# Head pairs mixed side by side in column tiles, and q cast straight into DRAM scratch, in a one-core Sinkhorn-attention and SwiGLU kernel

## The chip, the cores and the metric

The kernel runs on one core of one Trainium2 chip. The metric is device time in microseconds (us); lower is better. The runs of the kernel before scatter over about 2%. A run more than 1.5% above the fastest of its kernel counts as slow, and comparisons use fast runs alone.

Names of engines: PE is TensorE, DVE is VectorE, ACT is ScalarE, POOL is GpSimd, SP ("sync") is SyncE. DMAs issued by SP go through the hardware queue; those issued by POOL, which are the ones that cast fp32 to bf16, go through the software queue.

## The reference, cut to what matters

```python
B, H, S, D = 4, 8, 768, 64;  n_blocks = 8;  block = 96
P = sort_net                                   # (B, H, 8, 8); five rounds of exp and row/column normalisation
k_sorted = einsum('bhij,bhjcd->bhicd', P, k_blocks)      # each block becomes a mix of the 8 blocks
v_sorted = einsum('bhij,bhjcd->bhicd', P, v_blocks)
attn = softmax(q_block @ k_sorted_block.T / 8) @ v_sorted_block      # within a block of 96
x = attn heads side by side                    # (3072, 512)
out = (silu(x @ w_gate) * (x @ w_val)) @ w_out # d_ff 1536
```

## The kernel before, the parts that matter

The work runs in eight windows, two halves (of 384 tokens) for each of four batches. A window does the gate and value matmuls of its half, then the output matmuls of the half before; the attention of the next half and the preparation of the next batch are woven in between. Batch 0 is prepared by PE alone. Batches 1 to 3 go through DRAM scratch: k and v are mixed on PE (64 partitions each, one per head and block), written to scratch, and come back transposed by DMA (`kqt`, for k and q) or re-laid (`vt`, the value tile).

```python
def load_later(b):                                        # POOL, casts fp32 -> bf16
    load(kv[b][0:R], k_nat[b]); load(kv[b][R:2 * R], v_nat[b])
    for two in range(2):
        load(q_sb[b][two * 32:(two + 1) * 32], qv[two])
load_later(1); load(wo_sb, wo_dram); load_later(2); load_later(3)

def later_q(b):                                           # sync: q from SBUF to scratch, runs of 128 B
    qs = dram.tile([H2, NB, C, 2, D], BF16)
    for two in range(2):
        nc.sync.dma_start(out=qs[:, :, :, two]..., in_=q_sb[b][two * 32:(two + 1) * 32])

def one(c0, c):                                           # later_mix: 12 matmuls of 128x512 a batch
    nc.tensor.matmul(mp, lhsT=kvmix[b], rhs=kv[b][:, c:c + 8, :], ...)
    drain(m_sb[:, c - c0:c - c0 + 8], mp)                 # DVE and ACT in turn
    if c + 8 == c0 + CB:                                  # sync: k and v to scratch, runs of 128 B
        ...

def later_back(b):                                        # sync
    for a, t in ((1, "q"), (0, "k")):
        for g in range(H2):
            nc.sync.dma_start_transpose(out=kqt[:, a, g]..., in_=scr[(t, b)][g]...)
    nc.sync.dma_start(out=vt[:, :, 0:D], in_=scr[("v", b)]...)     # 6144 runs of 128 B
# ... cut ...
for w, (b, half) in enumerate(win):
    main = gv_steps(b, half)
    if w > 0: main = main + out_steps(*win[w - 1])
    if half == 0:
        sides.append((att_steps(b, 1), 0, n - 2))
        later_q(b + 1); sides.append((later_mix(b + 1), lo, lo + 6)); sides.append((later_back..., lo + 7, lo + 8))
    elif b + 1 < B:
        sides.append((att_steps(b + 1, 0), 1, n - 1))
    merge(main, *sides)
```

`merge` gives the order in which the program is written. A scheduler then reorders it when the kernel is built, by its own estimate of when each input is ready. PE executes that built order strictly: in the trace it stands 22.1 us at one matmul that waits, and does nothing that is written behind it.

The softmax here doesn't subtract the row's maximum and nothing guards it: scores larger than these inputs give would overflow.

Of the kernel before, what the change touches and what calls it, by code (L numbers as in the profile page):

```python
# [9 lines left out]
FP32 = mybir.dt.float32  # L10
BF16 = mybir.dt.bfloat16
AF = mybir.ActivationFunctionType
ALU = mybir.AluOpType
# [4 lines left out]
def kernel(  # L18
# [11 lines left out]
    nc = tc.nc  # L30

    B, H, S, D = q.shape
    NB = sort_net.shape[-1]
    C = S // NB
    BH = B * H
    H2 = H // 2
# [7 lines left out]
    R = H * NB  # L44
# [9 lines left out]
    const = ctx.enter_context(tc.tile_pool(name="const", bufs=1))  # L54
    natp = ctx.enter_context(tc.tile_pool(name="natp", bufs=1))
    mixp = ctx.enter_context(tc.tile_pool(name="mixp", bufs=2))
    kqp = ctx.enter_context(tc.tile_pool(name="kqp", bufs=2))
    vtp = ctx.enter_context(tc.tile_pool(name="vtp", bufs=2))
    epool = ctx.enter_context(tc.tile_pool(name="epool", bufs=8))
    ssp = ctx.enter_context(tc.tile_pool(name="ssp", bufs=3))  # L60
# [5 lines left out]
    psum = ctx.enter_context(tc.tile_pool(name="psum", bufs=3, space=bass.MemoryType.PSUM))  # L66
    dram = ctx.enter_context(tc.tile_pool(name="dram", bufs=1, space=bass.MemoryType.DRAM))
# [6 lines left out]
    kq0 = natp.tile([128, C, D], BF16, name="kq0", tag="nat", bufs=3)  # L74
    v0 = natp.tile([128, 128, D], BF16, name="v0")
    kv = [None] * B
    q23 = natp.tile([128, C, D], BF16, name="q23")
    q_sb = [None, v0[R:2 * R, 0:C], q23[0:R], q23[R:2 * R]]
    nc.vector.memset(v0[0:R, C:, :], 0.0)

    def load(dst, src):
        nc.gpsimd.dma_start(out=dst, in_=src)
# [25 lines left out]
    rmix = const.tile([128, 2, 2, H2, NB], BF16, name="rmix")  # L108
    vmix = const.tile([R, 2, H2, NB], BF16, name="vmix")

    kvmix = [None] + [const.tile([128, 2, 2, H2, NB], BF16, name=f"kvmix{b}") for b in range(1, B)]
    idq = ident[R:2 * R, R:2 * R].rearrange("p (g two j) -> p two g j", two=2, j=NB)
    nc.vector.memset(rmix, 0.0)
    nc.vector.tensor_copy(rmix[R:2 * R, :, 1, :, :], idq)
    for b in range(1, B):
        nc.vector.memset(kvmix[b], 0.0)

    for s in range(4):
        load(v0[s * 16:(s + 1) * 16, 0:C], v_nat[0, s * 16:(s + 1) * 16])
# [24 lines left out]
    for two in range(2):  # L144
# [1 line left out]
            rmix[0:R, two, 0],  # L146
            mask[0:R].rearrange("p (g two) -> p two g", two=2)[:, two].unsqueeze(2).to_broadcast([R, H2, NB]),
            wk, op=ALU.mult)
    nc.vector.tensor_copy(vmix, rmix[0:R, :, 0])
    for b in range(1, B):  # L150
        for t in range(2):
            rows = slice(t * R, (t + 1) * R)
            nc.vector.tensor_tensor(
                kvmix[b][rows, t].rearrange("p two g i -> p g two i"),
                mask[rows].rearrange("p (g two) -> p g two", two=2).unsqueeze(3).to_broadcast([R, H2, 2, NB]),
                w_ps[rows, :, b].unsqueeze(1).unsqueeze(1).to_broadcast([R, H2, 2, NB]), op=ALU.mult)

    for m in range(0, DF, 256):
        load(wg_sb[:, :, m:m + 256], wg_dram[:, :, m:m + 256])
        load(wv_sb[:, :, m:m + 256], wv_dram[:, :, m:m + 256])  # L160

    def load_later(b):
        kv[b] = natp.tile([128, C, D], BF16, name=f"kv{b}", tag="nat", bufs=3)
        load(kv[b][0:R], k_nat[b])
        load(kv[b][R:2 * R], v_nat[b])
        qv = q[b].rearrange("(g two) (j c) d -> two g j c d", two=2, c=C)
        for two in range(2):
            load(q_sb[b][two * 32:(two + 1) * 32], qv[two])

    load_later(1)  # L170
    load(wo_sb, wo_dram)
    load_later(2)
    load_later(3)

    tog = [0]

    def drain(dst, src):
        if tog[0] % 2 == 0:
            nc.vector.tensor_copy(dst, src)  # L179
        else:  # L180
            nc.scalar.copy(dst, src)  # L181
        tog[0] += 1
# [2 lines left out]

    def new_vt(b):

        vt = vtp.tile([C, H * NB, D + 1], BF16, name=f"vt{b}", tag="vt")
        nc.vector.memset(vt[:, :, D:D + 1], 1.0)
        vts[b] = vt  # L190
        return vt

# [15 lines left out]
            drain(dst[:, :, ts(cb, 8)], tp.transpose([0, 2, 1]))  # L208

    def first_v():  # L210
        dst = new_vt(0)
        for db in range(D // 8):
            tp = psum.tile([128, 8, H * NB], FP32, name="tv", tag="att")
            for ld in range(8):
                nc.tensor.matmul(tp[:, ld], lhsT=v0[0:R, :, db * 8 + ld],  # L215
                                 rhs=vmix.rearrange("p two g i -> p (two g i)"),
                                 start=True, stop=True)
            drain(dst[:, :, ts(db, 8)], tp[0:C].transpose([0, 2, 1]))



    scr = {}

    def later_q(b):
        qs = dram.tile([H2, NB, C, 2, D], BF16, name=f"qs{b}")
        for two in range(2):
            nc.sync.dma_start(out=qs[:, :, :, two].rearrange("g i c d -> (g i) c d"),
                              in_=q_sb[b][two * 32:(two + 1) * 32])
        scr[("q", b)] = qs

    def later_mix(b):

        ks = dram.tile([H2, NB, C, 2, D], BF16, name=f"ks{b}")
        vs = dram.tile([C, 2, H2, NB, D], BF16, name=f"vs{b}")
        scr[("k", b)], scr[("v", b)] = ks, vs
        steps = []
        CB = 48
        m_of = {}

        def one(c0, c):  # L240
            if c == c0:
                m_of[c0] = mixp.tile([128, CB, D], BF16, name="m_sb", tag="mix")
            m_sb = m_of[c0]
            mp = psum.tile([128, 8, D], FP32, name="mp", tag="att")
            nc.tensor.matmul(mp.rearrange("p a b -> p (a b)"),  # L245
                             lhsT=kvmix[b].rearrange("p a two g i -> p (a two g i)"),
                             rhs=kv[b][:, c:c + 8, :].rearrange("p a b -> p (a b)"),
                             start=True, stop=True)
            drain(m_sb[:, c - c0:c - c0 + 8], mp)
            if c + 8 == c0 + CB:  # L250
                for two in range(2):
                    nc.sync.dma_start(  # L252
                        out=ks[:, :, c0:c0 + CB, two].rearrange("g i c d -> (g i) c d"),
                        in_=m_sb[two * 32:(two + 1) * 32])
                nc.sync.dma_start(
                    out=vs[c0:c0 + CB].rearrange("c two g i d -> (two g i) c d"), in_=m_sb[R:2 * R])

        for c0 in range(0, C, CB):
            for c in range(c0, c0 + CB, 8):
                steps.append(lambda c0=c0, c=c: one(c0, c))  # L260
        return steps

    def later_back(b):
        kqt = new_kqt(b)
        for a, t in ((1, "q"), (0, "k")):
            s = scr[(t, b)].rearrange("g i c two d -> g (i c) (two d)")
            for g in range(H2):
                nc.sync.dma_start_transpose(out=kqt[:, a, g].rearrange("p i c -> p (i c)"), in_=s[g])  # L268
        vt = new_vt(b)
        nc.sync.dma_start(out=vt[:, :, 0:D],  # L270
                          in_=scr[("v", b)].rearrange("c two g i d -> c (two g i) d"))

    es_of = {}
    xts = {}
# [17 lines left out]
    def av(b, half, g):  # L292
        if g == 0:
            xts[(b, half)] = xtp.tile([128, H2, TW], BF16, name=f"xt{b}_{half}", tag="xt")
        xt, vt, es = xts[(b, half)], vts[b], es_of[(b, half, g)]
        av_ps = psum.tile([C, 2, 512], FP32, name="av_ps", tag="av", bufs=1)
        avv = av_ps[:, :, 0:4 * (D + 1)].rearrange("p two (i e) -> p two i e", e=D + 1)
        for two in range(2):
            for i4 in range(4):
                nc.tensor.matmul(avv[:, two, i4, :], lhsT=es[two][:, i4, :],  # L300
                                 rhs=vt[:, (two * H2 + g) * NB + half * 4 + i4, :],
                                 start=True, stop=True)
        r_sb = ssp.tile([C, 2, 4, 1], FP32, name="r_sb", tag="r")
        nc.vector.reciprocal(r_sb, avv[:, :, :, D:D + 1])  # L304
        st = ssp.tile([C, 4, 2, D], BF16, name="st", tag="st")
        nc.vector.tensor_tensor(st.rearrange("p i two d -> p two i d"), avv[:, :, :, 0:D],  # L306
                                r_sb.to_broadcast([C, 2, 4, D]), op=ALU.mult)
        x_ps = psum.tile([128, 4, C], BF16, name="x_ps", tag="att")
        for i4 in range(4):
            nc.tensor.transpose(x_ps[:, i4, :], st[:, i4].rearrange("p a b -> p (a b)"),  # L310
                                ident[0:C, 0:C])
        drain(xt[:, g, :], x_ps.rearrange("p a b -> p (a b)"))
# [78 lines left out]
    for w, (b, half) in enumerate(win):  # L391
        main = gv_steps(b, half)
        if w > 0:
            main = main + out_steps(*win[w - 1])
        n = len(main)
        sides = []
        if half == 0:
            sides.append((att_steps(b, 1), 0, n - 2))
            if b + 1 < B:
                later_q(b + 1)  # L400
                lo = 4 if w == 0 else 0
                sides.append((later_mix(b + 1), lo, lo + 6))
                sides.append(([lambda b=b: later_back(b + 1)], lo + 7, lo + 8))
        elif b + 1 < B:
            sides.append((att_steps(b + 1, 0), 1, n - 1))
        merge(main, *sides)
# [30 lines left out]
```

## Time and profile before

| | before |
|---|---|
| median of 3 runs | 323.8 us (323.37 to 324.45) |
| span of the profiled run | 321.9 us |
| PE restarts with batch 1's scores / first values of batch 1 are used | 108.95 us / 123.07 us |
| values to the end | 198.8 us |

In the page's slices (40 of about 8 us; busy tenths, and for PEclk the granted clock in tenths of full speed) PE has a hole from about 87 to 123 us, and the DMA engines are nearly full until about 80 us, at 7 tenths in most of the hole, and full again at its end, while the values are loaded:

```profile
PE   0377999999700105999999999999999799999995
...
PEclk9995579999955555599999999999999769999999
DMA  6999999999777799028799432697971000020022
```

The list of PE's waits (engine, instruction, what it waited for: us in total, times, longest) names what ended the hole: first the transposed k of batch 1, then its value tile. The line between them lies in the start of the program and is 12.5 us.

```profile
PE qk_1054 L284 <- DMA kqt_1011<-ks_666: 22.1, 1, 22.1
PE w_ps L140 <- DVE lmix L134: 12.5, 1, 12.5
PE av_ps L300 <- DMA vt_1020<-vs_667: 12.1, 1, 12.1
```

Sync's own timeline (start, us, engine, line, operation) shows the series behind it. The first issue waits for q's load until 52.8 us; its two stores of q are accepted only by 85.3 us, because the issuing queue is held while the DMA engines are busy with the loads. The mixed k and v, ready at about 61 us, stand behind them.

```profile
52.83 32.46 SPq L227 DMA_DIRECT2D qs_663<-v_99  x2
85.40 5.22 SPq L252 DMA_DIRECT2D ks_666<-m_sb  x2
90.67 0.99 SPq L255 DMA_DIRECT2D vs_667<-m_sb  x1
91.76 4.10 SPq L252 DMA_DIRECT2D ks_666<-m_sb  x2
95.90 1.58 SPq L255 DMA_DIRECT2D vs_667<-m_sb  x1
97.58 7.78 SPq L268 DMA_TRANSPOSE kqt_1011<-qs_663  x4
105.47 5.18 SPq L268 DMA_TRANSPOSE kqt_1011<-ks_666  x4
110.70 0.62 SPq L270 DMA_DIRECT2D vt_1020<-vs_667  x1
```

The two queues' packets (count, MB, share of the 16 engines' time), and the value loads of batches 1 to 3 (KB, us from issue to landing):

```profile
q1 hardware_dynamic: 96864, 20.46, 43.2%
q0 software_dynamic: 10000, 14.16, 29.2%
...
vt_1020<-vs_667 SPq DMA_DIRECT2D x1, 768.0 KB, 12.3
vt_1678<-vs_1404 SPq DMA_DIRECT2D x1, 768.0 KB, 12.7
vt_2463<-vs_2189 SPq DMA_DIRECT2D x1, 768.0 KB, 12.8
```

The last view cuts the time behind the arrival of the values into four stages: to the fifth attention step of batch 1 (the first of its second half), to that of batch 2, to that of batch 3, and to the end. Columns: stretch, length, busy us of each engine with counts, granted clock, DMA share and GB/s.

```profile
123.10:136.20 13.10, 11.82 (x88) 6.92 (x88) 5.98 (x13) 4.71 (x11) 0.00 (x0) 0.50 0.44 75
136.20:196.50 60.30, 59.25 (x438) 33.27 (x437) 36.60 (x75) 26.18 (x56) 0.00 (x0) 1.00 0.73 105
196.50:259.90 63.40, 61.55 (x441) 34.45 (x439) 36.50 (x74) 26.61 (x57) 0.00 (x0) 0.94 0.61 88
259.90:321.90 62.00, 58.17 (x356) 31.17 (x352) 29.54 (x58) 19.58 (x40) 0.00 (x0) 0.97 0.10 39
```

### The profile page before, as it was taken

How to read it: one execution, taken by the hardware profiler on the slowest of the kernel's cores; microseconds unless marked ns; L12 is line 12 of the kernel's file. 1: busy time of each engine (PE TensorE's matmuls, PEld its weight loads, DVE VectorE, ACT ScalarE, POOL GpSimd, SP SyncE). 2: the span in 40 equal slices, each digit the busy share in tenths (PEclk: the TensorE clock that was granted, in tenths of full speed). 3: DMA queues.
4: the chain of work that ended last, by engine and by line, in shares of the span. 5: the costliest groups of instructions: out<-in, count | busy, mean ns of one | idle time of the engine just before them, and what ended most of it. 6: DMA issues, size and time to landing. Idle time of an engine off the chain costs nothing.

```text
span 321.9 us, 5048 instructions
## 1 busy us (share of the span) xinstructions
PE 261.3 (81%) x2004; PEld 150.9 (47%) x2004; DVE 163.7 (51%) x353; ACT 112.9 (35%) x234; POOL 23.9 (7%) x43
## 2 busy tenths in 40 slices
PE   0377999999700105999999999999999799999995
PEld 0367555555300103556555555554554556555542
DVE  6844368888000002578438447890880558628600
ACT  2153346433200201455233346632333345333321
POOL 8554301000000000000000000000000000000000
PEclk9995579999955555599999999999999769999999
DMA  6999999999777799028799432697971000020022
GB/s 106 193 180 200 217 143 148 192 188 171 124 122 140 141 92 199 0 38 132 144 117 112 107 105 38 101 124 149 98 122 65 35 0 3 0 98 2 0 98 98
DMA packets 106886, 34.93 MB, mean 109 GB/s; under 512 B 94960, under 2 KB 102640, under 8 KB 106224
## 3 DMA queue, kind: packets, MB, share of 16 engines
q1 hardware_dynamic: 96864, 20.46, 43.2%
q0 software_dynamic: 10000, 14.16, 29.2%
q8 instruction: 15, 0.25, 0.3%
q14 instruction: 7, 0.06, 0.1%
HBM read 30.68 MB, written 13.37 MB: 137 GB/s over the span
## 4 chain that ended last, share of the span: by engine, by line
PE 76%; DMA 8%; SPq 7%; DVE 4%; ACT 2%; issue 1%; POOL 0%; ACTq 0%; POOLq 0%
PE v_ps L343 20%; PE o_ps L354 19%; PE g_ps L334 19%; PE av_ps L300 5%; SPq L268 4%; DMA vt_1020<-vs_667 4%; PE x_ps L310 3%; PE mp L245 3%; DVE st L306 3%; DMA v_99<-in_v_dram 2%; SPq L252 2%; PE tv L215 2%; DMA kq_98<-in_k_dram 1%; PE tkq L205 1%; DVE r_sb L304 1%
## 5 line engine op out<-in xcount | busy, mean ns | idle before, releaser
L339 DVE SCALAR_TENSOR_TENSOR gs_sb<-th_sb,g_ps 128x384 bf16<-128x384 bf16 x96 | 52.9, 553 | 39.0 <-ACT th_sb L337 34.4
L337 ACT ACTIVATE th_sb<-g_ps 128x384 bf16<-128x384 f32 x96 | 47.0, 492 | 60.6 <-PE g_ps L334 59.0
L343 PEld LDWEIGHTS <-wv_sb 128*128 128x128 bf16 x384 | 37.5, 99 | 26.9 <-issue 2.5
L334 PEld LDWEIGHTS <-wg_sb 128*128 128x128 bf16 x384 | 37.3, 102 | 24.8 <-issue 3.7
L304 DVE RECIPROCAL r_sb<-av_ps 96x8 f32<-96x8 f32 x32 | 6.4, 201 | 71.0 <-PE av_ps L300 70.9
L357 ACT COPY o_sb<-o_ps 128x512 f32<-128x512 f32 x24 | 14.1, 586 | 46.8 <-PE o_ps L354 46.8
L306 DVE TENSOR_TENSOR st<-av_ps,r_sb 96x512 bf16<-96x512 f32 x32 | 21.9, 684 | 0.8
L284 PE MATMUL qk_1054<-kqt_1011 64*96 64x96 bf16 x4 | 0.6, 286 | 22.1 <-DMA kqt_1011<-ks_666 22.1
L310 PE MATMUL x_ps<-ident,st 96*128 96x96 bf16 x128 | 12.4, 228 | 4.2 <-DVE st L306 3.7
L310 PEld LDWEIGHTS <-st 96*128 96x128 bf16 x128 | 8.3, 106 | 15.3 <-DVE st L306 13.8
L284 PEld LDWEIGHTS <-kqt_1011 64*96 64x96 bf16 x64 | 3.0, 158 | 25.4 <-DMA kqt_1011<-ks_666 23.6
L334 PE MATMUL g_ps<-xt_0_558,wg_sb 128*128 128x384 bf16 x48 | 13.7, 373 | 0.1
L179 DVE CAST m_sb<-mp 128x512 bf16<-128x512 f32 x18 | 12.0, 683 | 3.4 <-PE mp L245 3.1
L334 PE MATMUL g_ps<-xt_0_2682,wg_sb 128*128 128x384 bf16 x48 | 12.9, 364 | 0.7 <-ACT o_sb L357 0.6
L334 PE MATMUL g_ps<-xt_0_1112,wg_sb 128*128 128x384 bf16 x48 | 12.9, 357 | 0.0
L343 PE MATMUL v_ps<-xt_0_558,wv_sb 128*128 128x384 bf16 x48 | 12.1, 361 | 0.1
L181 ACT CAST m_sb<-mp 128x512 bf16<-128x512 f32 x18 | 10.6, 590 | 4.4 <-PE mp L245 4.4
L343 PE MATMUL v_ps<-xt_0_2682,wv_sb 128*128 128x384 bf16 x48 | 11.5, 355 | 0.0
L334 PE MATMUL g_ps<-xt_0_1897,wg_sb 128*128 128x384 bf16 x48 | 11.2, 325 | 0.1
L343 PE MATMUL v_ps<-xt_0_1112,wv_sb 128*128 128x384 bf16 x48 | 11.2, 343 | 0.0
L140 PE MATMUL w_ps<-selb,lmix 32*64 32x4 bf16 x16 | 0.6, 190 | 12.5 <-DVE lmix L134 12.5
L343 PE MATMUL v_ps<-xt_0_1897,wv_sb 128*128 128x384 bf16 x48 | 10.4, 326 | 0.0
(368 smaller groups left out, 446.2 us busy)
## 6 DMA issues: line engine op xcount, KB each, us to landing
out_dram<-o_sb SPq DMA_DIRECT2D x24, 256.0 KB, 2.0
wg_sb<-in_moe_w_gate_dram POOLq DMA_DIRECT2D x6, 256.0 KB, 10.6
wv_sb<-in_moe_w_val_dram POOLq DMA_DIRECT2D x6, 256.0 KB, 10.5
wo_sb<-in_moe_w_out_dram POOLq DMA_DIRECT2D x1, 1536.0 KB, 30.9
q_100<-in_q_dram POOLq DMA_DIRECT2D x4, 384.0 KB, 33.8
kq_98<-in_k_dram POOLq DMA_DIRECT2D x4, 192.0 KB, 5.9
kq_98<-in_q_dram POOLq DMA_DIRECT2D x4, 192.0 KB, 6.8
v_99<-in_v_dram POOLq DMA_DIRECT2D x4, 192.0 KB, 9.5
```

What stands on the lines that cost most here:

```text
L179: nc.vector.tensor_copy(dst, src)
L181: nc.scalar.copy(dst, src)
L268: nc.sync.dma_start_transpose(out=kqt[:, a, g].rearrange("p i c -> p (i c)"), in_=s[g])
L300: nc.tensor.matmul(avv[:, two, i4, :], lhsT=es[two][:, i4, :], rhs=vt[:, (two * H2 + g) * NB + half * 4 + i4, :], start=True, stop=True)
L306: nc.vector.tensor_tensor(st.rearrange("p i two d -> p two i d"), avv[:, :, :, 0:D], r_sb.to_broadcast([C, 2, 4, D]), op=ALU.mult)
L310: nc.tensor.transpose(x_ps[:, i4, :], st[:, i4].rearrange("p a b -> p (a b)"), ident[0:C, 0:C])
L334: nc.tensor.matmul(g_ps, lhsT=wg_sb[:, kc, ts(m, 128)], rhs=xt[:, kc, :], start=(kc == 0), stop=(kc == NKC - 1))
L337: nc.scalar.activation(th_sb, g_ps, AF.Tanh, scale=0.5)
L339: nc.vector.scalar_tensor_tensor(gs_sb, th_sb, 1.0, g_ps, op0=ALU.add, op1=ALU.mult)
L343: nc.tensor.matmul(v_ps, lhsT=wv_sb[:, kc, ts(m, 128)], rhs=xt[:, kc, :], start=(kc == 0), stop=(kc == NKC - 1))
L354: nc.tensor.matmul(o_ps, lhsT=h_w[:, m, ts(t3, 128)], rhs=wo_sb[:, m, :], start=(m == 0), stop=(m == NFC - 1))
L357: nc.scalar.copy(o_sb, o_ps)
```

## The change

Intent: fewer small DMA pieces and no q store in sync's way. Mixing leaves each head pair side by side, so a k or v row of scratch is one run of 6 KB; q is cast by its load straight into DRAM scratch; the value load has 256 B runs. For this, mixing uses four column tiles of 32 per PSUM bank.

```diff
-    load(q_sb[b][two * 32:(two + 1) * 32], qv[two])
+    qs = dram.tile([H2, S, 2, D], BF16, name=f"qs{b}")
+    load(qs[:, :, two].rearrange("g s d -> s g d"), qv[two])          # 6144 pieces: 256 B read, 128 B written
-    later_q(b + 1)                                                    # the q stores on sync are gone
 # later_mix
-    nc.tensor.matmul(mp..., lhsT=kvmix[b]... , rhs=kv[b][:, c:c + 8, :]...)
-    drain(m_sb[:, c - c0:c - c0 + 8], mp)
+    for two in range(2):
+        for t in range(4):
+            c = t * CT + s * 8
+            nc.tensor.matmul(mp[t * 32:(t + 1) * 32]..., lhsT=kvmix[b][rows, two]..., rhs=kv[b][rows, c:c + 8, :]...)
+        drain(m_sb[:, s * 8:s * 8 + 8, two], mp)
+    for t in range(4):                                                # once per k and per v: 32 rows of 6 KB
+        nc.sync.dma_start(out=sc[a, :, :, t * CT:(t + 1) * CT]..., in_=m_sb[t * 32:(t + 1) * 32]...)
 # later_back
-    vt [C, H * NB, D + 1];  out=vt[:, :, 0:D]        (6144 runs of 128 B)
+    vt [C, H2 * NB, 2 * D + 2];  out=vt[:, :, 1:2 * D + 1]   (3072 runs of 256 B, rows of 260 B)
-    sides.append((later_back, lo + 7, lo + 8))
+    sides.append((later_back, lo + 6, lo + 7))
 # cut: mixing weights, first values, and the value matmuls follow the new layout
```

More of the change, by code (lines that the diff above doesn't have):

```diff
@@ L76 @@
     kv = [None] * B
-    q23 = natp.tile([128, C, D], BF16, name="q23")
-    q_sb = [None, v0[R:2 * R, 0:C], q23[0:R], q23[R:2 * R]]
     nc.vector.memset(v0[0:R, C:, :], 0.0)
@@ L109 @@
     vmix = const.tile([R, 2, H2, NB], BF16, name="vmix")
-    kvmix = [None] + [const.tile([128, 2, 2, H2, NB], BF16, name=f"kvmix{b}") for b in range(1, B)]
+    kvmix = [None] + [const.tile([128, 2, H2, NB], BF16, name=f"kvmix{b}") for b in range(1, B)]
+    mask2 = const.tile([128, 2, H2], BF16, name="mask2")
+    mrow = mask.rearrange("p (g two) -> p two g", two=2)
+    nc.vector.tensor_copy(mask2[0:R], mrow[0:R])
+    for two in range(2):
+        nc.vector.tensor_copy(mask2[R:2 * R, two], mrow[R:2 * R, 1 - two])
     idq = ident[R:2 * R, R:2 * R].rearrange("p (g two j) -> p two g j", two=2, j=NB)
@@ L114 @@
     nc.vector.tensor_copy(rmix[R:2 * R, :, 1, :, :], idq)
-    for b in range(1, B):
-        nc.vector.memset(kvmix[b], 0.0)
     for s in range(4):
@@ L148 @@
             wk, op=ALU.mult)
-    nc.vector.tensor_copy(vmix, rmix[0:R, :, 0])
+    for two in range(2):
+        nc.vector.tensor_copy(vmix[:, two], rmix[0:R, 1 - two, 0])
     for b in range(1, B):
-        for t in range(2):
-            rows = slice(t * R, (t + 1) * R)
-            nc.vector.tensor_tensor(
-                kvmix[b][rows, t].rearrange("p two g i -> p g two i"),
-                mask[rows].rearrange("p (g two) -> p g two", two=2).unsqueeze(3).to_broadcast([R, H2, 2, NB]),
-                w_ps[rows, :, b].unsqueeze(1).unsqueeze(1).to_broadcast([R, H2, 2, NB]), op=ALU.mult)
+        nc.vector.tensor_tensor(
+            kvmix[b], mask2.unsqueeze(3).to_broadcast([128, 2, H2, NB]),
+            w_ps[:, :, b].unsqueeze(1).unsqueeze(1).to_broadcast([128, 2, H2, NB]), op=ALU.mult)
     for m in range(0, DF, 256):
@@ L160, with load_kv @@
         load(wv_sb[:, :, m:m + 256], wv_dram[:, :, m:m + 256])
-    def load_later(b):
+    scr = {}
+    def load_kv(b):
         kv[b] = natp.tile([128, C, D], BF16, name=f"kv{b}", tag="nat", bufs=3)
@@ L165, in load_later, with load_q @@
         load(kv[b][R:2 * R], v_nat[b])
-        qv = q[b].rearrange("(g two) (j c) d -> two g j c d", two=2, c=C)
+    def load_q(b):
+        qs = dram.tile([H2, S, 2, D], BF16, name=f"qs{b}")
+        qv = q[b].rearrange("(g two) s d -> two s g d", two=2)
         for two in range(2):
-            load(q_sb[b][two * 32:(two + 1) * 32], qv[two])
-    load_later(1)
+            load(qs[:, :, two].rearrange("g s d -> s g d"), qv[two])
+        scr[("q", b)] = qs.rearrange("g (i c) two d -> g i c two d", c=C)
+    load_kv(1)
+    load_q(1)
     load(wo_sb, wo_dram)
-    load_later(2)
-    load_later(3)
+    for b in range(2, B):
+        load_kv(b)
+        load_q(b)
     tog = [0]
@@ L186, in new_vt @@
     def new_vt(b):
-        vt = vtp.tile([C, H * NB, D + 1], BF16, name=f"vt{b}", tag="vt")
-        nc.vector.memset(vt[:, :, D:D + 1], 1.0)
+        vt = vtp.tile([C, H2 * NB, 2 * D + 2], BF16, name=f"vt{b}", tag="vt")
+        nc.vector.memset(vt[:, :, 0:2 * D + 2:2 * D + 1], 1.0)
         vts[b] = vt
@@ L210, in first_v @@
     def first_v():
-        dst = new_vt(0)
+        dst = new_vt(0)[:, :, 1:2 * D + 1].rearrange("c gi (two d) -> c two gi d", two=2)
         for db in range(D // 8):
@@ L217, in first_v @@
                                  start=True, stop=True)
-            drain(dst[:, :, ts(db, 8)], tp[0:C].transpose([0, 2, 1]))
-    scr = {}
-    def later_q(b):
-        qs = dram.tile([H2, NB, C, 2, D], BF16, name=f"qs{b}")
-        for two in range(2):
-            nc.sync.dma_start(out=qs[:, :, :, two].rearrange("g i c d -> (g i) c d"),
-                              in_=q_sb[b][two * 32:(two + 1) * 32])
-        scr[("q", b)] = qs
-    def later_mix(b):
-        ks = dram.tile([H2, NB, C, 2, D], BF16, name=f"ks{b}")
-        vs = dram.tile([C, 2, H2, NB, D], BF16, name=f"vs{b}")
-        scr[("k", b)], scr[("v", b)] = ks, vs
-        steps = []
-        CB = 48
-        m_of = {}
-        def one(c0, c):
-            if c == c0:
-                m_of[c0] = mixp.tile([128, CB, D], BF16, name="m_sb", tag="mix")
-            m_sb = m_of[c0]
-            mp = psum.tile([128, 8, D], FP32, name="mp", tag="att")
-            nc.tensor.matmul(mp.rearrange("p a b -> p (a b)"),
-                             lhsT=kvmix[b].rearrange("p a two g i -> p (a two g i)"),
-                             rhs=kv[b][:, c:c + 8, :].rearrange("p a b -> p (a b)"),
-                             start=True, stop=True)
-            drain(m_sb[:, c - c0:c - c0 + 8], mp)
-            if c + 8 == c0 + CB:
-                for two in range(2):
-                    nc.sync.dma_start(
-                        out=ks[:, :, c0:c0 + CB, two].rearrange("g i c d -> (g i) c d"),
-                        in_=m_sb[two * 32:(two + 1) * 32])
-                nc.sync.dma_start(
-                    out=vs[c0:c0 + CB].rearrange("c two g i d -> (two g i) c d"), in_=m_sb[R:2 * R])
-        for c0 in range(0, C, CB):
-            for c in range(c0, c0 + CB, 8):
-                steps.append(lambda c0=c0, c=c: one(c0, c))
-        return steps
@@ new lines, in first_v, with one @@
+            drain(dst[:, :, :, ts(db, 8)],
+                  tp[0:C].rearrange("c d (two gi) -> c two gi d", two=2))
+    def later_mix(b):
+        CT = C // 4
+        sc = dram.tile([2, H2, NB, C, 2, D], BF16, name=f"kvs{b}")
+        scr[("k", b)], scr[("v", b)] = sc[0], sc[1]
+        m_of = {}
+        def one(a, s):
+            rows = slice(a * R, (a + 1) * R)
+            if s == 0:
+                m_of[a] = mixp.tile([128, CT, 2, D], BF16, name="m_sb", tag="mix", bufs=3)
+            m_sb = m_of[a]
+            for two in range(2):
+                mp = psum.tile([128, 8, D], FP32, name="mp", tag="att")
+                for t in range(4):
+                    c = t * CT + s * 8
+                    nc.tensor.matmul(mp[t * 32:(t + 1) * 32].rearrange("p a b -> p (a b)"),
+                                     lhsT=kvmix[b][rows, two].rearrange("p g i -> p (g i)"),
+                                     rhs=kv[b][rows, c:c + 8, :].rearrange("p a b -> p (a b)"),
+                                     start=True, stop=True)
+                drain(m_sb[:, s * 8:s * 8 + 8, two], mp)
+            if s == CT // 8 - 1:
+                for t in range(4):
+                    nc.sync.dma_start(
+                        out=sc[a, :, :, t * CT:(t + 1) * CT].rearrange("g i c two d -> (g i) (c two d)"),
+                        in_=m_sb[t * 32:(t + 1) * 32].rearrange("p c two d -> p (c two d)"))
+        return [lambda a=a, s=s: one(a, s) for a in range(2) for s in range(CT // 8)]
@@ L269, in later_back @@
         vt = new_vt(b)
-        nc.sync.dma_start(out=vt[:, :, 0:D],
-                          in_=scr[("v", b)].rearrange("c two g i d -> c (two g i) d"))
+        nc.sync.dma_start(out=vt[:, :, 1:2 * D + 1],
+                          in_=scr[("v", b)].rearrange("g i c two d -> c (g i) (two d)"))
     es_of = {}
@@ L295, in av @@
         xt, vt, es = xts[(b, half)], vts[b], es_of[(b, half, g)]
-        av_ps = psum.tile([C, 2, 512], FP32, name="av_ps", tag="av", bufs=1)
-        avv = av_ps[:, :, 0:4 * (D + 1)].rearrange("p two (i e) -> p two i e", e=D + 1)
+        av_ps = psum.tile([C, 1024], FP32, name="av_ps", tag="av", bufs=1)
+        E = D + 1
         for two in range(2):
             for i4 in range(4):
-                nc.tensor.matmul(avv[:, two, i4, :], lhsT=es[two][:, i4, :],
-                                 rhs=vt[:, (two * H2 + g) * NB + half * 4 + i4, :],
+                o = i4 * E + (2 if two == 0 else 512)
+                lo = (1 - two) * E
+                nc.tensor.matmul(av_ps[:, o:o + E], lhsT=es[two][:, i4, :],
+                                 rhs=vt[:, g * NB + half * 4 + i4, lo:lo + E],
                                  start=True, stop=True)
-        r_sb = ssp.tile([C, 2, 4, 1], FP32, name="r_sb", tag="r")
-        nc.vector.reciprocal(r_sb, avv[:, :, :, D:D + 1])
+        sums = av_ps[:, 66:66 + 892].rearrange("p (two x) -> p two x", two=2)[:, :, 0:4 * E:E]
+        data = av_ps[:, 2:1024].rearrange("p (two x) -> p two x", two=2)[:, :, 0:4 * E].rearrange(
+            "p two (i e) -> p two i e", e=E)[:, :, :, 0:D]
+        r_sb = ssp.tile([C, 2, 4], FP32, name="r_sb", tag="r")
+        nc.vector.reciprocal(r_sb, sums)
         st = ssp.tile([C, 4, 2, D], BF16, name="st", tag="st")
-        nc.vector.tensor_tensor(st.rearrange("p i two d -> p two i d"), avv[:, :, :, 0:D],
-                                r_sb.to_broadcast([C, 2, 4, D]), op=ALU.mult)
+        nc.vector.tensor_tensor(st.rearrange("p i two d -> p two i d"), data,
+                                r_sb.unsqueeze(3).to_broadcast([C, 2, 4, D]), op=ALU.mult)
         x_ps = psum.tile([128, 4, C], BF16, name="x_ps", tag="att")
@@ L399 @@
             if b + 1 < B:
-                later_q(b + 1)
                 lo = 4 if w == 0 else 0
                 sides.append((later_mix(b + 1), lo, lo + 6))
-                sides.append(([lambda b=b: later_back(b + 1)], lo + 7, lo + 8))
+                sides.append(([lambda b=b: later_back(b + 1)], lo + 6, lo + 7))
         elif b + 1 < B:
```

## The prediction

> **What bounds the kernel now.** The slice table shows TensorE (PE) at 90% or more from about 40 to 87 us and from about 124 us to the end. Between lies a hole: the list of PE waits gives 22.1 us for batch 1's first transposed K (PE restarts at 108.95 us) and 12.1 us for its values (to 123.07 us). The granted clock is 0.50 from 92 to 136 us. Outside the hole and the start PE waits a few us, so the time is: arrival of batch 1's values (123) plus about 200 us of PE work.
>
> The chain of waits and the sync queue's waits say why. Sync issues its DMAs in order; the first is the scratch store of q, which waits 51.7 us for q's cast load, to 52.8 us. That store, 2 x 3072 runs of 128 B, takes until about 90 us because cast loads (wo, later k, v, q) run beside it until about 81 us; in batch 3 it lands in 5.8 us. The Trainium skill, "DMA: Bandwidth & Descriptors", section "Queues, rings and completion order", says an engine takes turns between queues packet by packet; the trace agrees. Mixed k and v, ready at 61 us, are issued only at 85.4 (12 us of stores), then eight transposes (13 us), then the value load (12.3 us).
>
> **What changes.** Gone: q stores from SBUF (6144 packets a batch), nearly all 12288 k/v store packets (now 256 rows of 6 KB), half of the value load's (3072 of 256 B). Added: q's cast load becomes 6144 pieces, 256 B read and 128 B written, DRAM to DRAM, on the load queue. From 16 ns per packet and engine of the 128 B stores and 27 ns of the value load I estimate 20 to 30 ns each: 8 to 12 us a batch against about 5; the load queue ends near 100 us, not 81. On PE, mixing is 48 matmuls a batch, not 12; if groups of four overlap (Trainium skill, "TensorEngine Tiling (Array Packing)", "Tiling Modes": tiles work in parallel; no run shows it yet) it costs 1 to 2 us a batch, if not, 8 us. Evictions stay 12 of 128x512 (683 ns DVE, 590 ns ACT). The built order puts batch 1's first scores inside window (0,1), its first values after 20 of 36 output matmuls.
>
> **On the critical path.** q lands near 55 us; its transposes, ahead of the k/v stores, share the engines with wo and k2/v2, to about 80; stores to 86; K transposed near 90; the value load competes with q2 and k3/v3 and lands near 112 (98 to 122). The 34 us hole shrinks to some 25. Behind it stay about 200 us, plus 3 us of output matmuls moved behind it, plus 3 us of mixing.
>
> **Predicted: 317 us, 300 to 331 (8 in 10).** Faster by over 2%: 0.55; within 2%: 0.33; slower by over 2%: 0.12.
>
> **What would show it.** PE waits for batch 1's K and values shorter than 22 and 12 us; values at 105 to 118 us; sync's wait for q followed by transposes; hardware-queue packets down from 96864 to about 33000, load-queue packets up from 10000 to about 28000; mixing matmuls starting in overlapping fours. Wrong: values later than 120 us.
>
> **What would make it wrong.** Cast pieces over 35 ns each (slower), or well under 20 ns, or transposes that do not crawl beside the loads (300 or less); column tiles one after another (+16 us); sync holding output stores behind q2's transposes.

## The result, and the profile after

| | before | after |
|---|---|---|
| median, 4 runs each | 324.12 us (323.37 to 327.03) | 307.56 us (304.15 to 313.85) |
| ratio of fast runs | | 0.9438, 95% interval 0.9331 to 0.9546 |
| span of the profiled run | 321.9 us | 306.2 us |
| first values of batch 1 used | 123.1 us | 115.0 us |
| values to the end | 198.8 us | 191.2 us |

A ratio is the mean time of one kernel's fast runs over that of the other's in the same rounds, so it is not quite the ratio of the medians. The changed kernel is faster by 5.6%; I had forecast 317 us, 2.2% less than the 324.12 us measured beside it. The 307.56 lies inside the stated range, but the gain is far above the one forecast, and that is the error to explain.

The same views of the changed kernel. The hole in PE's row now begins near 76 us, and after 122 us the clock stays at full speed; before, it fell again near 250 us.

```profile
PE   0367999999000859999999999999999999999994
...
PEclk9995579999755595999999999999999999999999
DMA  6999999999999995045994010489500200010022
```

```profile
PE qk_1089 L282 <- DMA kqt_1031<-kvs_664: 22.6, 1, 22.6
...
PE av_ps L301 <- DMA vt_1040<-kvs_664: 3.2, 1, 3.2
```

PE's wait for k did not get shorter (22.6 us, before 22.1), because the built order brings PE to it at 76.4 us, not at 86.9 us; the wait for values fell from 12.1 to 3.2 us. Sync now begins with q's transposes. They take 26 us, and the k/v stores stand behind them:

```profile
47.80 26.25 SPq L266 DMA_TRANSPOSE kqt_1031<-qs_216  x4
74.15 8.38 SPq L255 DMA_DIRECT2D kvs_664<-m_sb  x8
91.77 7.99 SPq L266 DMA_TRANSPOSE kqt_1031<-kvs_664  x4
99.93 0.46 SPq L268 DMA_DIRECT2D vt_1040<-kvs_664  x1
```

```profile
q0 software_dynamic: 27664, 14.16, 38.5%
q1 hardware_dynamic: 33120, 18.10, 37.2%
...
vt_1040<-kvs_664 SPq DMA_DIRECT2D x1, 768.0 KB, 15.1
vt_1699<-kvs_1435 SPq DMA_DIRECT2D x1, 768.0 KB, 10.2
vt_2518<-kvs_2254 SPq DMA_DIRECT2D x1, 768.0 KB, 11.2
```

Packets on the hardware queue fell to a third and those on the load queue rose to 27,664, as forecast. With half the pieces batch 1's value load got longer (15.1 us, before 12.3), and those of batches 2 and 3 only 2.5 and 1.6 us shorter. The stages behind the values:

```profile
115.00:129.80 14.80, 14.29 (x127) 7.87 (x127) 6.96 (x15) 6.46 (x14) 0.00 (x0) 0.79 0.31 91
129.80:188.90 59.10, 58.99 (x475) 31.91 (x473) 36.71 (x76) 26.97 (x56) 0.00 (x0) 1.00 0.52 95
188.90:246.80 57.90, 57.75 (x458) 31.62 (x456) 35.76 (x73) 25.89 (x54) 0.00 (x0) 1.00 0.44 83
246.80:306.20 59.40, 55.42 (x351) 29.86 (x348) 28.39 (x56) 19.53 (x39) 0.00 (x0) 0.99 0.11 40
```

Set against the table before, the 15.7 us between the two spans split up without rest: arrival of the values 8.1 us earlier; first stage 1.7 us longer (it holds 16 output matmuls that stood ahead of the hole before); second stage 1.2 us, third 5.5 us, fourth 2.6 us shorter. So about half of the gain lies behind the values, most of it in the last two stages, where the change altered, besides the mixing, only the layout of the value tile and of the value matmuls' results (the normalising operation on DVE takes 686 ns in both kernels).

What did alter there is the built order. In the kernel before, batch 3's first four value steps stand behind all 36 output matmuls of the window, nearly back to back (before them stand 130.6, 130.6, 131.0 and 131.5 us of gate, value and output matmuls, counted at N columns / 2.4 GHz each). In the changed kernel these four stand at 112.8, 115.2, 117.8 and 121.6 us, with 2.4 to 3.8 us of long matmuls between one and the next, which PE can run while DVE normalises the step. This clock rate is from the Trainium skill, "Trainium Kernel Development and Optimization", section "NeuronCore Architecture"; the trace agrees (four matmuls of 384 columns take 0.65 us in the chain).

### The profile page after: what moved, and what is told of

The parts are those of the page before. It is cut to its first block, busy times and chain, and to the rows that moved or that the text cites. A ratio compares the mean times of both kernels' runs of the same rounds, so it can differ in the third digit from the quotient of the medians.

```text
span 306.2 us, 5232 instructions
## 1 busy us (share of the span) xinstructions
PE 257.5 (84%) x2103; PEld 145.8 (48%) x2112; DVE 163.2 (53%) x351; ACT 114.6 (37%) x234; POOL 32.3 (11%) x43
## 3 DMA queue, kind: packets, MB, share of 16 engines
q0 software_dynamic: 27664, 14.16, 38.5%
q1 hardware_dynamic: 33120, 18.10, 37.2%
## 4 chain that ended last, share of the span: by engine, by line
PE 60%; DMA 23%; SPq 12%; POOL 2%; issue 1%; ACT 1%; DVE 0%; POOLq 0%; ACTq 0%
PE o_ps L358 19%; PE g_ps L338 15%; PE v_ps L347 15%; SPq L266 11%; DMA qs_216<-in_q_dram 5%; DMA kvs_664<-m_sb 5%; DMA vt_1040<-kvs_664 5%; PE av_ps L301 4%; DMA wg_sb<-in_moe_w_gate_dram 4%; DMA v_99<-in_v_dram 3%; PE mp L248 2%; PE x_ps L314 2%; POOL kq_98 L80 1%; POOL qs_216 L80 1%; SPq L255 0%
## 5 line engine op out<-in xcount | busy, mean ns | idle before, releaser
L347 PEld LDWEIGHTS <-wv_sb 128*128 128x128 bf16 x384 | 37.4, 99 | 26.3 <-issue 2.9
L338 PEld LDWEIGHTS <-wg_sb 128*128 128x128 bf16 x384 | 35.1, 100 | 25.7 <-issue 7.4
L349 DVE SCALAR_TENSOR_TENSOR h_1_1073<-v_ps,gs_sb 128x384 bf16<-128x384 f32 x12 | 6.7, 558 | 24.3 <-PE v_ps L347 23.4
L282 PE MATMUL qk_1089<-kqt_1031 64*96 64x96 bf16 x4 | 0.6, 286 | 22.6 <-DMA kqt_1031<-kvs_664 22.6
L338 PE MATMUL g_ps<-xt_0_559,wg_sb 128*128 128x384 bf16 x48 | 13.3, 358 | 0.1
L314 PE MATMUL x_ps<-ident,st 96*128 96x96 bf16 x128 | 11.7, 217 | 1.2 <-DVE st L310 1.0
L347 PE MATMUL v_ps<-xt_0_559,wv_sb 128*128 128x384 bf16 x48 | 11.8, 354 | 0.0
L347 PE MATMUL v_ps<-xt_1_724,wv_sb 128*128 128x384 bf16 x48 | 11.4, 362 | 0.0
L338 PE MATMUL g_ps<-xt_1_724,wg_sb 128*128 128x384 bf16 x48 | 11.2, 357 | 0.0
L338 PE MATMUL g_ps<-xt_0_1147,wg_sb 128*128 128x384 bf16 x48 | 10.8, 327 | 0.0
L358 PE MATMUL o_ps<-wo_sb,h_0_679 128*128 128x512 bf16 x34 | 10.3, 449 | 0.3 <-issue 0.2
L338 PE MATMUL g_ps<-xt_0_1966,wg_sb 128*128 128x384 bf16 x48 | 10.5, 327 | 0.0
```

The lines of the kernel that those rows point to most:

```text
L314: nc.tensor.transpose(x_ps[:, i4, :], st[:, i4].rearrange("p a b -> p (a b)"), ident[0:C, 0:C])
L338: nc.tensor.matmul(g_ps, lhsT=wg_sb[:, kc, ts(m, 128)], rhs=xt[:, kc, :], start=(kc == 0), stop=(kc == NKC - 1))
L347: nc.tensor.matmul(v_ps, lhsT=wv_sb[:, kc, ts(m, 128)], rhs=xt[:, kc, :], start=(kc == 0), stop=(kc == NKC - 1))
L358: nc.tensor.matmul(o_ps, lhsT=h_w[:, m, ts(t3, 128)], rhs=wo_sb[:, m, :], start=(m == 0), stop=(m == NFC - 1))
```

## The experiments

Theories at the start: A, the built order and the density of PE's work set the time behind the values. B, the attention steps became cheaper by the new layout or by less DMA traffic.

### Order moved in the kernel before (spread3)

```diff
-    sides.append((att_steps(b + 1, 0), 1, n - 1))
+    sides.append((att_steps(b + 1, 0), 11, 15) if b == 2 else (att_steps(b + 1, 0), 1, n - 1))
+    # and each main step of that window is kept behind the value matmuls written before it
```

> The kernel before, with one thing changed: PE's order is held so that batch 3's first attention half lies between the last gate/value matmuls and the output matmuls of the window before it, instead of behind all of them. No DMA and no arithmetic changes. Theory A (what the prediction missed is PE work behind the values running at full clock instead of half, because dense matmuls stand between the attention steps): the stretch that ran at clock 0.62 for 12 us near 250 us goes to 0.95 or more, and the time falls by 4 to 7 us, to 317 to 320 us (ratio about 0.98 to 0.985). Rival B (the attention steps themselves became cheaper in the changed kernel, or less DMA traffic made them faster): nothing of that is in this kernel, so 324 us within 1 us.

Measured: 318.15 us, inside the stated 317 to 320; ratio 0.9865 (0.9764 to 0.9966), which alone does not settle a gain of 2%. The third and fourth stage (stages as above):

```profile
197.20:256.70 59.50, 58.52 (x443) 32.91 (x444) 37.69 (x76) 26.63 (x57) 0.00 (x0) 1.00 0.66 94
256.70:316.00 59.30, 55.35 (x347) 29.86 (x348) 28.33 (x55) 19.53 (x39) 0.00 (x0) 0.99 0.11 40
```

Values arrive as before (123.6 us). The stages are 59.5 and 59.3 us, where the kernel before has 63.4 and 62.0: together 6.6 us of the 8.1 us by which the change shortened them, by order alone. The clock is at 1.00 and 0.99. The other 1.5 us this run does not explain.

### Order moved back in the changed kernel (cluster3)

```diff
-    elif b + 1 < B:
+    elif b + 1 < B and b != 2:
         sides.append((att_steps(b + 1, 0), 1, n - 1))
     merge(main, *sides)
+    if b == 2 and half == 1:          # issued behind the last output matmul
+        run(att_steps(3, 0))
```

> The changed kernel, with PE's order held so that batch 3's first attention half stands behind all output matmuls of the window before it, as it stood in the kernel before. All DMAs and arithmetic are those of the changed kernel. Theory A: the cold stretch comes back there (a granted clock near 0.6 for about 10 us where the changed kernel has 1.0) with 2 to 3 us of idle PE, and the time grows by 4 to 7 us over the changed kernel, to 311 to 315 us. Rival B: the same as the changed kernel within 1 us.

Measured: 316.24 us median of four runs, two of them slow; the fast ones 312.32 and 314.08 us, ratio 0.9707 (0.9542 to 0.9873).

```profile
185.50:248.90 63.40, 61.09 (x455) 33.31 (x453) 35.51 (x71) 25.78 (x54) 0.00 (x0) 0.93 0.42 76
248.90:310.10 61.20, 57.24 (x351) 30.90 (x352) 29.37 (x58) 19.48 (x40) 0.00 (x0) 0.97 0.11 39
```

The stages are back at 63.4 and 61.2 us, 7.3 us more than in the changed kernel. The fast runs lie in the stated 311 to 315 us. Beside the changed kernel's fast runs of the same rounds (303.06 and 300.45 us) the growth is larger than the 4 to 7 us forecast; the scatter of the runs is in that difference, so the stage lengths are the cleaner measure. B predicted no change in either run, and fell.

### The changed kernel again (after2)

> The changed kernel once more, to stand beside the others on the same chip, and for a second trace. Both theories: about 304 to 310 us; values of batch 1 at about 115 us; the clock at 1.0 from about 121 us to the end if that was no accident of one run.

Measured: fast runs 303.06 and 300.45 us, below the stated 304 to 310 (slow ones 309.67 and 307.99 us), ratio 0.9353 (0.9177 to 0.9528). The trace fell in a slow run and still has the order's mark: values at 116.7 us, and clock 0.9 or more in every slice of the page from 123 us on.

### Is it the clock at the hole's end? (warm1)

```diff
+    f1 = filler(92, last_o[0])        # 92 matmuls of 128x512 in PE's wait for k
     qk(1, 0, 0); qk(1, 0, 1)
+    f2 = filler(48, last_qk[0])       # 48 in its wait for values
     av(1, 0, 0) ...                   # batch 3's order held as in the kernel before
```

> The kernel before, with 92 filler matmuls of 128x512 on PE in the wait for batch 1's K and 48 in the wait for its values; their results are not read. Values still arrive near 123 us. Theory A: PE is kept at full clock through the hole, so the 13.9 us behind the values that ran at clock 0.51 run at 1.0; the time falls by about 5 to 6 us, to 317 to 320 us. Rival B: the hole's end sets everything, the time stays at 324 us, or grows by whatever the filler delays.

Measured: 327.06 us, ratio 1.0133 (0.9974 to 1.0293). The clock stayed at 1.00 in the first wait, the values came at 125.6 us, and the first stage took 12.3 us at a mean clock of 0.63, against 13.1 us at 0.50 before: PE had only 10.55 us of work in it and the clock fell again. So my forecast of 5 to 6 us was wrong and rival B right: starting warm shortened that stage by 0.8 us. What full clock through the whole stage would be worth is not shown, since the filler did not bring it about. My reading is that the clustered steps lack other work for PE and that the low clock comes with that; A holds in the form that spread3 and cluster3 show. The second stage took 62.7 us here, before 60.3; why was not looked into. This kernel also issues one of batch 3's q stores earlier on sync, which the comparison carries.

### The two parts alone (q_only, q_only2, mix_only)

q_only is the kernel before with the q part of the diff; mix_only is the changed kernel with q's old way through SBUF and two mixing buffers instead of three.

> The kernel before with the q part of the change alone: q cast straight into DRAM scratch; mixing, its 128 B stores and the value load stay as before. Theory C (values of batch 1 come when three things in series are through: q's way to scratch, the k/v stores, transposes and value load; each part of the change takes a piece, and batch 3's attention moves ahead of the output matmuls in either): sync's transposes of q begin near 48 us, the k/v stores still take over 10 us, values land at 116 to 121 us; the time is 313 to 318 us. Rival D (only the 6 KB stores matter, q's route is worth nothing): values at 123 us, and only what the order of batch 3 gives, 317 to 320 us.

> q_only once more, for a trace of a fast run: values of batch 1 at 118 to 126 us by theory C; at 128 us or later the q part alone brings the values no earlier than before, and its gain is all behind the values.

> The changed kernel with q loaded into SBUF and stored to scratch by sync as before; column-tiled mixing, 6 KB runs, 256 B value load as changed (two mixing buffers instead of three, for space). Theory C: q's store still blocks sync until about 85 us, then the k/v stores take 4 us instead of 12 and the value load 10 instead of 12: values at 112 to 117 us; batch 3's attention stands ahead of the output matmuls as in the changed kernel; 308 to 313 us. Rival E (sync being blocked by q's store is what counts, so nothing is gained without the q part): values at 121 us or later, 317 us or more.

| | time, us | ratio (95%) | values of batch 1 | values to end |
|---|---|---|---|---|
| q_only | 316.02 | 0.9785 (0.9667 to 0.9904) | 130.5 (slow run) | 189.8 |
| q_only2 | 320.98, one run | | 130.6 | 188.3 |
| mix_only | 314.56 | 0.975 (0.9633 to 0.9867) | 118.8 | 193.6 |
| both (the change) | 307.56 | 0.9438 | 115.0 | 191.2 |

The q part alone brings the values no earlier in either trace; there they come 7 us later. Sync's timeline of q_only2 shows why: q's transposes take 33 us, and the small k/v stores then need 29 us.

```profile
48.24 33.21 SPq L261 DMA_TRANSPOSE kqt<-qs  x4
81.54 7.07 SPq L245 DMA_DIRECT2D ks<-m_sb  x2
88.66 9.30 SPq L248 DMA_DIRECT2D vs<-m_sb  x1
98.06 9.11 SPq L245 DMA_DIRECT2D ks<-m_sb  x2
107.22 3.24 SPq L248 DMA_DIRECT2D vs<-m_sb  x1
```

Its gain is all behind the values: the built order also moves batch 3's attention, to the last gate and value matmuls and the first output matmuls. So of the two theories for q_only, C met the time but missed the arrival (116 to 121 us), and D was right that the values come no earlier, but put them at 123 us, some 7 us too early, and the time 1 us too high (317 to 320 us, measured 316.02; the single run of q_only2 is 320.98). For mix_only, C named the direction, but the arrival of 118.8 us and the time of 314.56 us are each about 2 us above its ranges; E, which gave the mixing part no worth, falls. The two parts together bring the values earlier than the mixing part alone, though the q part alone does not. My reading, not tested by a run of its own: the slow transposes push the small k/v stores to where later loads run beside them, and only large stores can make that up. In q_only2's packet records the stores share the engines with loads and casts until about 110 us (from 94 to 98 us, 322 packets against 319); in the kernel before they ran when the loads had all but ended.

### What keeps batch 1 late (loads_late, late_q, late_all, before_late)

The transposes of 128x768 take 1.28 us each when nothing runs beside them (before: 5.18 us for four). In the changed kernel q's four take 26 us beside the loads of later batches. These kernels hold loads of batches 2 and 3 on POOL until batch 1's value tile has landed:

```diff
+    g = nc.gpsimd.tensor_copy(gate[:, 0:8], vts[1][0:1, 0, 0:8])     # POOL waits here for batch 1's values
+    # issued behind it: loads_late (gated by copies into the load targets): k, v of batches 2, 3 (q was meant too, but its casts were built ahead of it)
+    #                   late_q: q casts of batches 2, 3;  late_all: k, v and q;  before_late: the same in the kernel before
```

> The changed kernel, but the loads of batches 2 and 3 (k, v and q) are held on the GpSimd queue until batch 1's value tile has landed; everything else as changed. Theory F (the loads of later batches on the same DMA engines make batch 1's transposes, stores and value load crawl): q's four transposes take under 12 us instead of 26, values of batch 1 land at 75 to 88 us, PE's wait for K falls from 22.6 to under 5 us, and the time falls to 278 to 288 us. Rival G (the chain of issues on sync, store after transposes after q, is what takes the time, whatever runs beside it): values not before 100 us, 296 us or more.

> The changed kernel with only the q casts of batches 2 and 3 held behind batch 1's value tile; k and v of batches 2 and 3 (12 KB packets) run early, as changed. Theory F1 (the long packets of the k and v loads are what q's transposes wait behind): q's transposes still take 20 us or more, values land at 95 to 106 us, 288 to 299 us. Theory F2 (the small cast pieces are what slows them): q's transposes under 14 us, values before 92 us, under 287 us.

> As loads_late, where the q casts of batches 2 and 3 turned out to run early all the same; now they too are held behind batch 1's value tile. Theory F: q's transposes share the engines with the output weights alone and are through by about 62 us, the k/v stores by about 67, K by 73, the values land near 82 us, just as PE gets to them; PE waits under 4 us in all there, and the time is 274 to 281 us. Rival: the held loads come too late for batch 2's mixing, PE waits there, and nothing is gained over loads_late (282 us or more).

> The kernel before, with the loads of batches 2 and 3 held behind batch 1's value tile; no other part of the change. Theory F (company on the DMA engines is the main cause of the hole, more than the number of small packets): q's 6144-packet store takes about 10 us instead of 37, the stores are through by about 75 us, values land at 96 to 104 us, batch 3's attention stays behind the output matmuls; 297 to 306 us, as good as the whole change. Rival H (128 B packets as such are the cause): values at 112 us or later, 312 us or more.

| | time, us | ratio (95%) | q's transposes | values of batch 1 |
|---|---|---|---|---|
| the change | 307.56 | 0.9438 | 26.3 us | 115.0 |
| late_q | 296.66 | 0.9176 (0.9077 to 0.9275) | 33.1 us | 103.1 |
| loads_late | 283.79 | 0.8826 (0.8731 to 0.8921) | 9.8 us; two of batch 2 until 68.9 us | 91.8 |
| late_all | 284.35 | 0.8837 (0.8762 to 0.8912) | 8.9 us | 85.1 |
| before_late | 306.87 | 0.9512 (0.9432 to 0.9593) | 9.1 us | 97.0 |

Sync's timelines of late_q, loads_late (its first 10 us) and late_all:

```profile
47.57 33.06 SPq L273 DMA_TRANSPOSE kqt<-qs  x4
```

```profile
47.58 9.79 SPq L275 DMA_TRANSPOSE kqt<-qs  x4
```

```profile
47.20 8.90 SPq L272 DMA_TRANSPOSE kqt<-qs  x4
56.20 7.21 SPq L261 DMA_DIRECT2D kvs<-m_sb  x8
...
100.44 10.07 SPq L272 DMA_TRANSPOSE kqt<-qs  x4
110.63 8.21 SPq L261 DMA_DIRECT2D kvs<-m_sb  x8
```

With the casts gone and the k and v loads left, the transposes crawl as before (33.1 us, F1); with the k and v loads gone and the casts left they take 9.8 us, and with both gone 8.9 us. The packet records show how: those loads move in packets of 12,288 B that take 926 ns each (median), and a transpose's 256 B packets wait their turn between them. In the changed kernel the load queue and the hardware queue move nearly equal numbers of packets there, for example 34 and 35 from 56 to 58 us, 30 and 31 in the next 2 us. The Trainium skill, "DMA: Bandwidth & Descriptors", section "Queues, rings and completion order", says that an engine takes turns between its queues packet by packet; these counts agree. before_late shows that company, not the number of small packets, makes most of the hole in the kernel before: with not one small packet taken away it is about as fast as the change (0.9512 against 0.9438). Its time is 0.9 us above its range, and its second stage is long (72.6 us, before 60.3): the held loads put off batch 2's chain, whose values PE waits 4.9 us for. loads_late met F's time, but its values came at 91.8 us and not by 88: two of batch 2's transposes were built ahead of batch 1's stores, and sync waited there for batch 2's q cast until 66.4 us.

late_all met F for the transposes and values, and lost it again: batch 2's q transposes begin only at 100.44 us and its stores at 110.63 us, so its values come at 136.4 us and PE waits 6.1 us for them, so the rival named beside it was right about the time.

### Stores moved to the ACT queue (kv_on_act)

```diff
-    nc.sync.dma_start(out=sc[a, ...
+    nc.scalar.dma_start(out=sc[a, ...
```

> The changed kernel with the k/v stores issued from the ACT queue, so that they no longer stand behind q's transposes on sync. Theory F: stores issue near 55 and 60 us, but everything still crawls beside the loads; values of batch 1 land at 95 to 108 us, 290 to 300 us. Rival G: the 26 us in which the stores stood behind the transposes are the whole delay, so values land before 92 us and the time is under 288 us.

Measured: 340.29 us, ratio 1.0471 (1.034 to 1.0603), slower; neither theory. Without the stores sync's built order put batch 2's q transposes ahead of batch 1's k (eight transposes until 94.0 us). Four of the stores stood on ACT from 72.43 us for 27.67 us, in which it did none of its own work. That was not issuing: each took 0.32 us. By the trace's semaphore records the second to the fourth waited for semaphores that those transposes raise, since this program uses the same few DMA semaphores for both queues. The list of ACT's waits names them:

```profile
ACT th_sb L341 <- DMA kqt<-qs: 39.8, 1, 39.8
```

So this run does not separate F from G.

### Holding loads in two steps, and aligned value rows (late_split, vt_aligned, split_aligned)

```diff
 # late_split
+    g = nc.gpsimd.tensor_copy(gate[:, 0:8], kqts[1][0:1, 0, H2 - 1, 0, 0:8])   # batch 1's k is transposed
+    #   behind it: q cast of batch 2
+    g = nc.gpsimd.tensor_copy(gate[:, 8:16], vts[1][0:1, 0, 0:8])              # batch 1's values have landed
+    #   behind it: k, v of batches 2 and 3, q cast of batch 3
 # vt_aligned
-    vt = vtp.tile([C, H2 * NB, 2 * D + 2], BF16, ...);   out=vt[:, :, 1:2 * D + 1]     # rows of 260 B
+    vt = vtp.tile([C, H2 * NB, 2 * D + 32], BF16, ...);  out=vt[:, :, 16:2 * D + 16]   # rows of 320 B, runs start on 32 B
```

> The changed kernel with the loads of batches 2 and 3 held in two steps: batch 2's q cast until batch 1's K has been transposed, all the others until batch 1's values have landed. If late_all lost its gain because batch 2's q came last (sync stood before q's transposes until 100 us there), batch 1's values land near 85 us and batch 2's at 128 to 132 us instead of 136 us, PE waits under 8 us in all for values, and the time is 274 to 280 us. If it is batch 2's k and v that come too late, batch 2's values stay at 135 us or later and the time at 282 us or more.

> The changed kernel with 15 elements of padding in each row of the value tile, so that the 256 B runs of the value load start on multiples of 32 B in SBUF (rows of 320 B instead of 260 B). Theory J (it is the odd start of each run that keeps the value load at 10 to 15 us though the change halved its pieces): the loads of batches 2 and 3 fall from 10.2 and 11.2 us to under 7 us, batch 1's from 15.1 to under 12 us. Rival K (the order in which it reads scratch, or company, sets it): unchanged within 1 us, and 300 to 309 us in all.

> late_split and vt_aligned together. By J another 3 to 4 us earlier values for batch 1 and batch 2, 270 to 277 us; by K the same as late_split.

| | time, us | ratio (95%) | values of batch 1 / 2 | PE waits for values |
|---|---|---|---|---|
| late_split | 278.97 | 0.8634 (0.8591 to 0.8677) | 85.2 / 132.8 | 2.4 us |
| vt_aligned | 302.44 | 0.9285 (0.9198 to 0.9371) | 110.9 / 155.9 | none listed |
| split_aligned | 276.2 | 0.8542 (0.8494 to 0.8591) | 86.1 / 131.1 | none listed |

```profile
vt<-kvs SPq DMA_DIRECT2D x3, 768.0 KB, 7.3
```

The value loads of vt_aligned take 11.7, 6.5 and 7.3 us for batches 1 to 3; in the changed kernel they take 15.1, 10.2 and 11.2 us with the same pieces from the same scratch. Beside equal company the same is seen: 10.3 to 11.3 us in late_split, 5.9 to 6.7 us in split_aligned. J holds (it had said under 7 us for the last two), and K falls. The time of vt_aligned, 302.44 us, does not stand clear of the changed kernel's scatter. late_split met its time, and its values for batch 2 came 0.8 us later than stated. In split_aligned, the fastest kernel here and correct, batch 1's values are in time for PE, so the faster load shows only in batch 2, by 1.7 us, where J had said 3 to 4 us for both; the time, 2.8 us less than late_split's, lies in J's range.

## Why the prediction was right or wrong

- **What bounds it: right in part.** "Arrival of batch 1's values plus about 200 us of PE work" is how the time adds up, but the second term was read as fixed.
- **The failed step: "Behind it stay about 200 us", plus 3 and 3.** That makes 206 us; the runs show 191.2 us, 14.8 us less. The 198.8 us of before held a cold third and fourth stage (clock 0.94 and 0.97, PE idle 1.9 us in the third) that belong to batch 3's clustered attention. The built order moved, and with it 8.1 us of these two stages; spread3 and cluster3 move 6.6 and 7.3 us by order alone. The two additions were too large as well: the first stage, with the output matmuls moved behind the values, grew by 1.7 us only, at a mean clock of 0.79 and not 0.50, and the second, with most of batch 2's mixing, became 1.2 us shorter. I had read batch 1's place in the built order and not batch 3's.
- **Values near 112 us (98 to 122): right,** 115.0 and 116.7 us. Its parts erred against each other. q landed at 47.7 us, not 55: the cast pieces took 13 ns each per engine while they ran nearly alone (some 2,400 in 2 us on 16 engines, by the packet records), not 20 to 30. The transposes then took until 74 us to issue, and PE got k at 99 us, not near 90. That transposes crawl beside the loads was right, and late_q with loads_late names the loads: k and v (33.1 us with them, 9.8 us without).
- **The value load with half its pieces: worth less than the change intended.** The prediction gave no time for it. It took 15.1 us beside the loads, and 10.2 and 11.2 us later, against 12.3 to 12.8 us. vt_aligned took off another 3.4 to 3.9 us, so here where the runs start (with the row length, which changed with it) cost more than their number.
- **The hole: right in size,** 34.2 to 25.8 us of listed waits. "PE waits for batch 1's K shorter than 22 us" was wrong (22.6): PE came to it 10 us earlier.
- **Column tiles: right.** Eight mixing matmuls of 512 columns take 0.55 us from the first to the next instruction, at 48.65 us in PE's timeline of the changed kernel, so 0.27 us for four. The Trainium skill, "TensorEngine Tiling (Array Packing)", section "Tiling Modes", says tiles of one array work in parallel; the trace agrees.
- **Packet counts: right,** 33,120 and 27,664.

Left open: why runs of the changed kernel scatter by some 4% (300.45 to 313.85 us), why either part of the change alone moves batch 3's attention in the built order, and how the 5.5 us of the third stage split between PE's empty slots and the clock.

## What to carry to other kernels

Before calling the part behind a stall fixed, compare the built order of the whole program, not of the stalled spot alone, and look at the clock there: short dependent steps set back to back cost more here than the same steps between long matmuls. When a chain of small DMAs is late, first look at what runs beside it; holding loads that nobody needs yet was worth about as much in the kernel before as the whole change (0.9512 against 0.9438), and brought the changed kernel on to 0.8634. Before counting the pieces of a load into SBUF, try an aligned start for each run; here it was worth more than halving them.

## What the Trainium skill lacked or had wrong

- "DMA: Bandwidth & Descriptors", section "SWDGE vs HWDGE vs iDMA", gives a packet as at most 4096 B "preferably". The k and v cast loads here show 12,288 B in a packet record, 926 ns each, and the page has no figure for what such company costs a small-packet DMA: four transposes took 8.9 to 9.8 us without them and 26 to 33 us beside them.
- The same page has no time for where a run starts in SBUF on the write side of a load: a load of 3072 runs of 256 B into rows of 260 B took 10.2 to 15.1 us, and with starts on 32 B, in rows of 320 B, 6.5 to 11.7 us.
- "TensorE: Matmul & The Clock Gate", part 1, gives the clock back after about 3.4 us of sustained work. In the first stage before, PE was busy 11.82 of 13.1 us, as the profile counts it, and the granted clock stayed at 0.50. That work is short matmuls and transposes with gaps between them; how much of it counts as sustained, part 1 does not say.
